# Where a small load is issued: x and the gate's weights in one load ahead of the context's end, or in two behind it

## The chip, the cores and the metric

The kernel runs on one core of a Trainium2 chip. Its time is the device time of one execution in microseconds; three runs of the kernel before gave a median of 773.87 us (773.8 to 774.09). The profile is of one execution, and its span goes from the first to the last recorded instruction.

## What is computed

Two rows x (B = 2, one token each, D = 1024) go through two branches, and a gate mixes them:

```
g   = sigmoid((x * gate_w).sum(-1))
a   = attention(x @ wq, k_cache, v_cache) @ wo     # 32 query heads, 4 kv heads, 32768 keys, head size 128
b   = x + gelu(layernorm(x) @ w3) @ w4              # what is left of the mixer with one token
out = g * a + (1 - g) * b
```

With a single token the shifted mixing of the reference is a sum over zeros, so w1 and w2 are not read. All data are float32. The caches are by far the most of it: 2 x 4 pairs of batch row and kv head, each with 16 MB of keys and 16 MB of values.

## The kernel before

Everything large passes through two buffers of 128 partitions x 64 KB, `ring` (also `flat`, the same memory with flat rows). SP issues every large load, in one written order: wq in two halves, w3 in two halves, then for each of eight pairs two halves of keys and two of values (w4 in two halves ahead of the fifth pair), last wo in four pieces and the `tail` in four. `load` (L212) puts a wait in front of the issue where the buffer must first come free: w3's halves wait for the marks `q0` and `q1` (L249, L250), which PE sets when it has multiplied with the halves of wq.

The only other input is `xg`, 128 partitions x 24 floats: on each partition 8 values of each of the two rows of x and 8 of gate_w. It goes to `xg_sb`. ACT issues its load (L245) inside a critical block (L242 to L245), in which SP also issues the two halves of wq. `tc.close()` and `tc.compile()` (L246, L247) end the tile context; all engines meet there, and the rest of the program is written engine by engine with semaphores set by hand.

What x sets going, in order:

- DVE waits for `got_x` at 16 (L307), forms x * gate_w and the sums over k (L308 to L310).
- PE waits for it too (L338), permutes x (L340) and sums over partitions with a matrix of ones (L344); DVE writes `x_run` and `x_pad` (L315, L319), the mean and the squares (L321 to L325); PE sums again (L346).
- ACT loads the table of its square root ahead of that (L329), then computes the root and the gate's sigmoid (L329, L330); DVE writes `xn_pad` and `xr_pad` for layernorm and the residual.
- PE then runs `project(x_pad, ...)` (L383, matmuls in `columns`, L355): for each half of wq it waits until that half has landed (L361), does 32 matmuls of 512 columns (64 instructions in the profile, each a pair), and marks the end, `q0` and `q1`.

So x stands ahead of PE's use of wq's first half, that use ahead of the mark `q0`, and that mark ahead of SP's issue of w3's first half (L249).

A DMA raises its semaphore by 16 when it has landed. `got_x` is used a second time at the end: the first two pieces of `tail` raise three of these semaphores again, and `came` (L210) holds the values that PE waits for there, 32 for `got_x`.

Of the kernel before, what the change touches and what calls it, by code (L numbers as in the profile page):

```python
# [14 lines left out]
P = 128  # L15
B, D, HQ, HKV, SK, DH, F = 2, 1024, 32, 4, 32768, 128, 3584
REP = HQ // HKV
PAIRS = B * HKV
# [53 lines left out]
def kernel(  # L72
# [52 lines left out]
    nc = tc.nc  # L125
    scale = DH ** -0.5

    def new(name, *shape, parts=P):
        return nc.alloc_sbuf_tensor(name, [parts, *shape], F32).ap()
# [6 lines left out]
    xg_sb = new("xg_sb", KD, 3)  # L136
# [55 lines left out]
    def sem(name):  # L192
        cleared.append(nc.alloc_semaphore(name))
        return cleared[-1]

    stored = nc.alloc_semaphore("stored")
    pe, dve, act, pool = (Line(e, sem(n)) for e, n in (
        (nc.tensor, "pe"), (nc.vector, "dve"), (nc.scalar, "act"), (nc.gpsimd, "pool")))
# [4 lines left out]
    got_x = sem("got_x")  # L203
# [3 lines left out]
    step, own_step, to_pe, pt_in, b_in, e_in, x_in, k1_free = (  # L207
        sem(n) for n in ("step", "own_step", "to_pe", "pt_in", "b_in", "e_in", "x_in", "k1_free"))

    came = ((got_x, 32), (b_in, 16), (pt_in, 16), (k1_free, PAIRS + 16))  # L210

    def load(dst, src, sem, *marks):  # L212
        sp.after(*marks)
        nc.sync.dma_start(dst, src).then_inc(sem, 16)  # L214

    def run(src, j):
        return src[PART * j:PART * (j + 1)].rearrange("i (q w) c -> (i q) (w c)", w=PART)
# [24 lines left out]
    with tc.tile_critical(sync_engine=mybir.EngineType.SP):  # L242
        for j in range(2):
            load(flat[j], run(wq, j), landed[j])
        nc.scalar.dma_start(xg_sb, xg).then_inc(got_x, 16)  # L245
    tc.close()  # L246
    tc.compile()  # L247

# [26 lines left out]
        load(tail[:, 3 * D + i * D // 2:3 * D + (i + 1) * D // 2], run(wo, 1)[:, lo:lo + D // 2], came[2 + i][0])  # L275


    pool.mark(nc.gpsimd.memset(wide, 0.0))
    pool.after((pool.sem, pool.n))
    made = pool.mark(nc.gpsimd.affine_select(  # L280
# [11 lines left out]
    def then(inst):  # L292

        mark = dve.mark(inst)
        dve.after(mark)
        return mark
# [5 lines left out]
    d_perm = dve.mark(last)  # L302
# [1 line left out]
    def over_k(t):  # L304
        return t.rearrange("p (o b) -> p o b", o=1).to_broadcast([P, KD, B])

    dve.after((got_x, 16))  # L307
    then(nc.vector.tensor_mul(xw, xs, xg_sb[:, :, B:B + 1].to_broadcast([P, KD, B])))  # L308
    nc.vector.tensor_reduce(part[:, 0:B], xw.rearrange("p k b -> p b k"), axis=AX.X, op=ALU.add)
    d_part = dve.mark(nc.vector.tensor_reduce(  # L310
# [24 lines left out]
    then(nc.vector.tensor_scalar(rest, gate, -1.0, 1.0, op0=ALU.mult, op1=ALU.add))  # L335
    d_norm = dve.mark(nc.vector.tensor_mul(xr_pad[:, :, ::C // B], xs, over_k(rest)))

    pe.after(d_perm, (got_x, 16))  # L338
    for w in range(PART):
        last = nc.tensor.matmul(tr[1][:, w * KD * B:(w + 1) * KD * B], perm[:, w].rearrange("p i q -> p (i q)"), xs,  # L340
                                start=True, stop=True)
# [314 lines left out]
```

## Time and profile before

| | |
|---|---|
| time, median of 3 runs | 773.87 us |
| profiled execution, its time | 773.87 us |
| its span | 772.3 us |
| PE busy | 431.1 us (56%) |
| DVE busy | 94.6 us (12%) |
| ACT busy | 60.8 us (8%) |
| read from HBM | 331.36 MB, 429 GB/s over the span |

The page gives busy time by engine, 40 slices of the span with the share in tenths, the DMA queues, the chain of work that ended last, and the costliest groups of instructions. In the DMA view a queue's row has its packets, MB and the time that they took as a share of 16 engines over the window asked for; it can be over 100% in a short window, since a packet counts where it starts. In the timeline a row has its start, its length, engine, line, operation, tiles and count, and in brackets the idle time before it and what ended that. "SPq" and "ACTq" are the issues of DMAs, not their transfers.

### The profile page before, as it was taken

The page shows a single profiled execution, that of the slowest core. Times are in us where ns is not written, and L with a number is a line of the kernel's source. Part 1 is how long each engine was busy: PE and PEld are TensorE (multiplying, and loading weights), DVE is VectorE, ACT ScalarE, POOL GpSimd, SP SyncE. Part 2 cuts the span into 40 slices and gives each one's busy share as a digit, 9 for nine tenths or more (in the row PEclk, how much of TensorE's full clock was granted, in tenths as well). Part 3 has the DMA queues.
Part 4 walks back from the last instruction along what each step waited for, and adds up shares of the span by engine and source line. Part 5 has one row for each costly group of instructions (what it writes and reads, how often), then busy time and mean ns, then how long its engine had stood idle before and what let it go on. Part 6 is the DMA issues. An engine that isn't in the chain of part 4 may idle for free. (4 is left out here: it accounts for less than half of the span.)

```text
span 772.3 us, 7548 instructions
## 1 busy us (share of the span) xinstructions
PE 431.1 (56%) x3380; PEld 198.3 (26%) x3380; DVE 94.6 (12%) x267; ACT 60.8 (8%) x145; POOL 3.6 (0%) x12
## 2 busy tenths in 40 slices
PE   1465746454745474656475347454656464547476
PEld 0131413222322232323232113122323131213234
DVE  2010102100210021002100002100210021002110
ACT  1000002000200021002000002000200020002000
POOL 1000000000000000000000000000000000000000
PEclk9976677877687668667867777776776787777779
DMA  9999999999999999999999999999999999999997
GB/s 381 435 435 435 435 435 435 435 429 431 431 435 431 435 435 435 435 435 435 430 428 443 429 435 435 435 435 435 435 435 435 435 435 435 435 435 435 418 426 325
DMA packets 6805, 331.51 MB, mean 429 GB/s; under 512 B 900, under 2 KB 908, under 8 KB 1292
## 3 DMA queue, kind: packets, MB, share of 16 engines
q1 hardware_dynamic: 6634, 331.36, 99.3%
q8 instruction: 8, 0.13, 0.1%
q10 hardware_dynamic: 162, 0.02, 0.0%
q14 instruction: 1, 0.01, 0.0%
HBM read 331.36 MB, written 0.01 MB: 429 GB/s over the span
## 5 line engine op out<-in xcount | busy, mean ns | idle before, releaser
L471 PE MATMUL sc<-load,q_cur 128*32 128x512 f32 x1024 | 146.9, 734 | 133.0 <-PEq L51 133.0
L497 PE MATMUL pv<-load,pt 128*32 128x512 f32 x1024 | 130.9, 669 | 90.3 <-PEq L51 90.3
L471 PEld LDWEIGHTS sc<-load,q_cur 128*32 128x32 f32 x1024 | 52.7, 132 | 221.1 <-issue 219.3
L497 PEld LDWEIGHTS pv<-load,pt 128*32 128x32 f32 x1024 | 39.1, 122 | 172.1 <-issue 172.1
L488 PE MATMUL sc<-wide,p 128*128 128x128 f32 x256 | 44.3, 346 | 22.8 <-PEq L51 22.8
L554 DVE TENSOR_REDUCE mx<-sc 128x1 f32<-128x512 f32 x32 | 21.4, 689 | 287.0 <-PE sc L471 287.0
L538 ACT ACT_TABLE_LOAD x8 | 10.3, 1283 | 488.7 <-ACTq L51 488.7
L488 PEld LDWEIGHTS sc<-wide,p 128*128 128x128 f32 x256 | 39.9, 183 | 30.0 <-issue 30.0
L369 PE MATMUL acc<-load,w_pad 128*32 128x256 f32 x448 | 29.9, 428 | 19.6 <-PEq L51 19.6
L571 DVE COPY pt<-sc 64x256 f32<-64x256 f32 x64 | 25.9, 414 | 75.5 <-PE sc L488 75.0
L544 ACT COPY pt<-sc 64x256 f32<-64x256 f32 x64 | 23.5, 367 | 79.4 <-PE sc L488 77.1
L576 DVE COPY pv_sb<-pv 128x512 f32<-128x512 f32 x16 | 10.3, 686 | 149.6 <-PE tr L503 149.6
L355 PE MATMUL sc<-load,x_pad 128*32 128x512 f32 x128 | 17.9, 722 | 16.3 <-PEq L51 16.3
L369 PEld LDWEIGHTS acc<-load,w_pad 128*32 128x32 f32 x448 | 17.0, 123 | 31.7 <-issue 25.7
L507 PE MATMUL tr<-sel,pv_sb 128*128 128x8 f32 x128 | 18.6, 282 | 11.8 <-PEq L51 11.8
L355 PE MATMUL sc<-load,xn_pad 128*32 128x384 f32 (+1 forms) x128 | 17.4, 711 | 9.3 <-PEq L51 9.3
L538 ACT ACTIVATE p<-sc,bias 128x512 f32<-128x512 f32 x32 | 21.5, 685 | 0.1
L507 PEld LDWEIGHTS tr<-sel,pv_sb 128*128 128x128 f32 x128 | 18.1, 226 | 12.3 <-issue 12.3
L567 DVE COPY p<-p 128x256 f32<-128x256 f32 x32 | 9.4, 294 | 26.7 <-ACT p L538 26.7
L355 PEld LDWEIGHTS sc<-load,x_pad 128*32 128x32 f32 x128 | 5.0, 130 | 28.4 <-issue 28.4
L355 PEld LDWEIGHTS sc<-load,xn_pad 128*32 128x32 f32 x128 | 5.3, 139 | 21.5 <-issue 21.5
L340 PE MATMUL tr<-xg_sb,perm 128*128 128x16 f32 x4 | 1.0, 372 | 13.4 <-DMA xg_sb<-xg 13.4
(86 smaller groups left out, 92.4 us busy)
## 6 DMA issues: line engine op xcount, KB each, us to landing
load<-w SPq DMA_DIRECT2D x4, 7168.0 KB, 27.2
load<-wo SPq DMA_DIRECT2D x1, 7168.0 KB, 29.0
load<-wo SPq DMA_DIRECT2D x1, 4096.0 KB, 17.6
load<-wo SPq DMA_DIRECT2D x1, 2048.0 KB, 22.1
load<-wo SPq DMA_DIRECT2D x1, 1024.0 KB, 24.1
tail<-wo SPq DMA_DIRECT2D x1, 1024.0 KB, 26.1
tail<-wo SPq DMA_DIRECT2D x1, 512.0 KB, 26.9
tail<-wo SPq DMA_DIRECT2D x2, 256.0 KB, 27.1
```

The lines of the kernel that those rows point to most:

```text
L355: last = nc.tensor.matmul(b[C * g:C * g + C, :hi - lo], pad[:, k], t[:, o + lo:o + hi], start=(k == 0), stop=(k == KD - 1))
L369: inst = nc.tensor.matmul(acc[C * g:C * g + C], lhsT, rows[:, g * (D // G):(g + 1) * (D // G)], start=False, stop=last, skip_group_check=True)
L471: last = nc.tensor.matmul(sc[i][C * g:C * g + C], q_cur[:, w, s], ring[j][:, w, o:o + 512], start=(s == 0 and w == 0), stop=(s == 1 and w ...
L488: last = nc.tensor.transpose(sc[k][:, t * P:(t + 1) * P], pair.rearrange("p w q -> p (w q)"), ident)
L497: last = nc.tensor.matmul(pv[C * g:C * g + C], pt[j][w][:, lo:lo + C], ring[j][:, w, o:o + G * DH], start=(j == 0 and w == 0 and t == 0), ...
L507: last = nc.tensor.matmul(tr[1][:, w * REP:(w + 1) * REP], pv_sb[:, s, w].rearrange("p i q -> p (i q)"), sel[:, s], start=(s == 0), stop=( ...
L538: nc.scalar.activation(p[:, i, :, :PART], sc[i].rearrange("p (t q w) -> p t w q", t=NT, w=PART), AF.Exp, bias=bias, scale=scale, accum_out ...
L544: nc.scalar.copy(*halves(1, j, c)).then_inc(pt_in, 1)
L554: last = [nc.vector.reduce_max(out=mx[:, k:k + 1], in_=sc[k], axis=AX.X) for k in ((1, 2) if i == 2 else (i,))][-1]
L567: nc.vector.tensor_copy(p[:, i, :, PART], p[:, i, :, 0]).then_inc(to_pe, 1)
L571: nc.vector.tensor_copy(*halves(0, j, c)).then_inc(pt_in, 1)
L576: last = nc.vector.tensor_copy(pv_sb[:, :, :, i], pv.rearrange("p (s q w) -> p s w q", q=HALF, w=PART))
```

## The change

The load of `xg` leaves the critical block. Behind the end of the context, and behind the written list of SP's loads, ACT issues it as two loads, of partitions 0 to 119 and of 120 to 127, both on `got_x`. The waits for x go from 16 to 32, and the wait at the end on the same semaphore from 32 to 48. SP's list, the order of its loads and all instructions of PE, DVE and POOL are as before. On ACT the two issues now stand behind the context's end and ahead of the first table load.

```diff
-    came = ((got_x, 32), (b_in, 16), (pt_in, 16), (k1_free, PAIRS + 16))
+    came = ((got_x, 48), (b_in, 16), (pt_in, 16), (k1_free, PAIRS + 16))
...
     with tc.tile_critical(sync_engine=mybir.EngineType.SP):
         for j in range(2):
             load(flat[j], run(wq, j), landed[j])
-        nc.scalar.dma_start(xg_sb, xg).then_inc(got_x, 16)
     tc.close()
     tc.compile()
...
+    for rows in (slice(0, 120), slice(120, P)):
+        nc.scalar.dma_start(xg_sb[rows], xg[rows]).then_inc(got_x, 16)
...
-    dve.after((got_x, 16))
+    dve.after((got_x, 32))
...
-    pe.after(d_perm, (got_x, 16))
+    pe.after(d_perm, (got_x, 32))
```

## The prediction

> **What bounds the kernel now.** I read the page's totals and slices first, then the chain that ended last, then the first 51 us of the timeline, and last the DMA view in short windows, because the change touches only the start.
>
> ```profile
> span 772.3 us, 7548 instructions
> DMA  9999999999999999999999999999999999999997
> GB/s 381 435 435 435 435 435 435 435 429 431 431 435 431 435 435 435 435 435 435 430 428 443 429 435 435 435 435 435 435 435 435 435 435 435 435 435 435 418 426 325
> q1 hardware_dynamic: 6634, 331.36, 99.3%
> DMA tail<-wo 4%; PE pv L497 1%; SPq L214 0%; PE sc L378 0%; ACT out L619 0%
> ```
>
> The sixteen DMA engines are full from the first slice to the last: SP's queue q1 alone takes 99.3% of them. The chain ends in the last of its loads. So the time is the length of q1's stream, and an edit matters only if it makes that stream start at another time, run dry, or carry more. The first slice has 381 GB/s where the next ones have 435: 12% of 19.3 us, some 2.4 us at the start in which nothing moves yet.
>
> The x load is small and early. These rows of the timeline carry its way to the stream:
>
> ```profile
> 0.92 0.41 ACTq L245 DMA_DIRECT2D xg_sb<-xg  x1
> 0.96 0.88 SPq L214 DMA_DIRECT2D load<-wq  x2
> 2.91 1.28 ACT L329 ACT_TABLE_LOAD   x1 [2.91 <-PEq L247]
> 13.26 0.17 DVE L308 TENSOR_TENSOR xw<-xg_sb 128x16 f32<-128x16 f32 x1 [6.57 <-DMA xg_sb<-xg]
> 15.94 0.59 PE L346 MATMUL tr<-part,ones 128*128 128x2 f32 x2 [1.16 <-DVE part L325]
> 23.00 9.53 PE L355 MATMUL sc<-load,x_pad 128*32 128x512 f32 x64 [6.48 <-PEq L51]
> 32.59 18.55 SPq L214 DMA_DIRECT2D load<-w  x2
> 42.37 8.39 PE L355 MATMUL sc<-load,x_pad 128*32 128x512 f32 x64 [9.83 <-PEq L51]
> ```
>
> x can be used at 13.26. From there to the end of L346 it takes 15.94 + 0.59 - 13.26 = 3.27 us; PE then idles 6.48 us until wq's first half is there at 23.00. It multiplies for 9.53 us, and its end (32.53) lets SP issue w3's first half at 32.59 into the buffer that came free.
>
> Now the DMA view in windows: what starts in 1.9:3.05, in 5.0:5.7 (the queues' rows of 7.4:8.1 and 9.8:10.5 have the same packets), in 12.3:12.9, in 21.9:22.6, in 41.2:41.9 and in 0:42. Each row of digits cuts its window into 40 slices, so a digit that isn't 0 says when packets start: in the second, slices 4 to 35 of 0.0175 us, 5.07 to 5.62. q10 is ACT's queue, and up to 42 us it carries nothing but x.
>
> ```profile
> q1 hardware_dynamic: 16, 1.05, 254.3%
> q10 hardware_dynamic: 80, 0.01, 10.9%
> ...
> DMA  0000900090000009099090909900990000090000
> ...
> q1 hardware_dynamic: 16, 1.05, 345.4%
> q10 hardware_dynamic: 16, 0.00, 1.7%
> ...
> DMA  0009000900000000990909090099009090000090
> ...
> q10 hardware_dynamic: 16, 0.00, 1.5%
> ...
> q1 hardware_dynamic: 32, 1.05, 346.7%
> ...
> DMA  0000000900009000009909099909900990000090
> ...
> q10 hardware_dynamic: 144, 0.01, 0.4%
> ```
>
> x is 144 packets: 128 rows and 16 completions, so 8 + 1 on each of 16 engines. 80 of them, five per engine, go beside the first 16 packets of wq; then comes one per engine each time that an engine ends a packet of wq: at 5.07 to 5.62, in 7.4:8.1, in 9.8:10.5, and its completions at 12.34 to 12.88 (slices 3 to 38 of 0.015 us). A packet of wq takes 3.454 x 16 x 0.7 / 16 = 2.418 us. So **a small packet that shares the engines with the stream waits 2.42 us for each turn**, and x was early only because five of its nine turns were over before the stream began, thanks to an issue 0.04 us ahead of SP's. In 21.9:22.6 q1 has 32 packets, 16 of data and the 16 completions of wq's first half. The last row of digits is the same for wq's second half: it ends between 41.32 and 41.88 (slices 7 to 38), and w3 must be there by then or the engines stand still.
>
> **The change, part by part.** *Removed:* one DMA issue (0.41 us) on ACT at 0.92. SP's two issues at 0.96 are in the same place and wait for nothing of ACT's. The 144 packets cost the engines 0.4% of 42 us = 0.17 us each, spent now or later. The first wq packets took 2.543 x 1.15 = 2.92 us in the mean against 2.418; if x's neighbourhood causes that, up to 0.5 us comes back, or nothing. I take 0.
>
> *Moved:* the load goes behind the context's end. There ACT's first instruction starts at 2.91 (the table load, L329). Both x issues stand ahead of that load now; it moves back by two issues, and its user waited long for it:
>
> ```profile
> 16.76 0.20 ACT L329 ACTIVATE rstd<-rstd 128x2 f32<-128x2 f32 x1 [12.57 <-DVE rstd L327]
> 770.50 1.11 ACTq L620 DMA_DIRECT2D out<-out  x1
> ```
>
> An issue on ACT costs 0.41 (x) to 1.11 us (the result's), so the two end at 3.7 to 5.1 and the table at 6.4 at the latest: hidden under 12.57 us of waiting, and uncovered only if the table took longer than x. DVE and PE have the same instructions, with a 32 for a 16 in two waits, and the tail's first wait (48 for 32) counts the same events: nothing.
>
> *What the move costs x.* Issue to first packet was about 1.05 us (0.92 to some 1.97; the window 1.9:2.0 holds 16 packets of x and none of wq):
>
> ```profile
> q10 hardware_dynamic: 16, 0.00, 9.7%
> ```
>
> So x's first packet can go at 2.91 + 1.05 = 3.96 or later, inside the first wq packet, which ends at 5.1 to 5.6. The head start is gone and every turn costs 2.42 us.
>
> How many turns? 120 rows on 16 engines put 8 rows on some (120/16 = 7.5), plus a completion: 9 turns. The 8-row load shares engines with them (9 + 1 + 1 = 11) unless it goes whole to an engine that the first one leaves free (again 9). x was spread as thinly as its rows allow, so I take 11; the other end is 9, that is 4.84 us less. The Trainium skill ("DMA: Bandwidth & Descriptors", section "Why a DMA increments its semaphore by 16 and not by 1") says that a copy runs on the largest number of engines up to 16 that divides its rows: by that, an estimate, 15 engines with 8 rows and 8 engines with one, which gives 11 as well.
>
> At which packet end does the first turn come? If an engine picks its next packet only as it ends one, at the first (5.1 to 5.6); if it has picked wq's second packet by 3.96 to 4.9, at the second. The stream runs without gaps although a first packet costs 0.5 us more, so picking is at least 0.5 us ahead; x comes 0.7 to 1.1 us ahead. The slowest of eight engines decides. I take the second end; the first and the third are the bounds. One turn is saved where q1's own completion comes between two wq packets (21.9:22.6), so eleven turns from the second end finish at the 2 + 9 = 11th: 5.6 + 10 x 2.42 = 29.8. With 13.26 - 12.88 = 0.38 us to DVE, x is usable at **30.2, 16.9 us later**.
>
> *What covers that.* First PE's idle time: 23.00 - 16.53 = 6.47 us. Then the lead of w3's issue: at 32.59, where the stream needs it by 41.32 - 1.05 = 40.27: 7.68 us. Together 14.15, that is, x usable by 27.4 costs nothing. So 16.9 - 14.15 = **2.8 us in which the engines stand dry**, and nothing gives that back, since the stream has no other hole. Two corrections bound it. After a dry spell the first packets may cost 0.5 us more again (up to 3.3). And PE's 9.53 us holds a slow beginning, as these two rows of its lines in 22.9:27 and 29:32 show:
>
> ```profile
> L355 PE MATMUL sc<-load,x_pad 128*32 128x512 f32 x20 | 4.5, 1059 | 6.5 <-PEq L51 6.5
> ...
> L355 PE MATMUL sc<-load,x_pad 128*32 128x512 f32 x36 | 4.0, 592 | 0.0
> ```
>
> After an idle spell a matmul takes 1059 ns, later 592. With the chain L340 to L346 right ahead of it PE may be quick sooner, as in the second half's 8.39: 1.1 us less (down to 1.7). Later work has room: wq's second half is multiplied at 43 instead of 42.37, and what follows waits for w3, which is later by the same 2.8.
>
> *Sum.* The profiled execution took 773.87 us (span 772.3), which is also the median of the three runs: 773.87 + 2.8 = **776.7 us**, with 775.5 to 777.3 for this case.
>
> **Rivals.**
>
> 1. *x's turns start one packet earlier* (first end, last turn 27.4, usable at 27.8): 0.4 us over the cover, minus up to 1.1, plus up to 0.5: 773.9 to 774.8. This is the case that is not slower, together with nine turns; it decides from x usable at 27.4, and the forecast lies 2.8 us on the wrong side of it. For it: an engine that picks late. Against: the stream's lack of gaps. 0.20, and 0.02 for nine turns.
>
> 2. *Several small packets go in one turn.* Five went together at the start. If that is no head start but a habit of the engines (five in a first turn, or in each), eleven packets take three to seven turns, the last at 5.6 + 7 x 2.42 = 22.6 at the latest, x is usable by 23.0, inside the cover, and the time stays: 773.5 to 774.0. Against: rounds two to four had one each, though the rest of x was surely queued. 0.13. The Trainium skill ("DMA: Bandwidth & Descriptors", section "Queues, rings and completion order") speaks for more of this: an engine drains a whole packet of typically 9 to 17 descriptors from one ring before it switches; by that x would be in within one turn. The trace does not agree: 16 packets of q10 per 16 packets of q1.
>
> 3. *Later still.* If the engines have picked two to four packets of wq ahead, the turns begin at the third to fifth end: 2.4 us more each, 779.1 to 784 (where rival 4 begins). Against: 256 KB picked ahead by each engine is much. 0.14, most of it at the third end.
>
> 4. *x stands behind wq's second half altogether*, if the packets of both queues reach the engines in the order of issue. x then comes when the stream runs dry, at 41.9, is usable at 42.3, and w3 is issued at 42.3 + 3.27 + 9.53 = 55.1: 42.3 - 27.4 = 14.9 us over, 784 to 789. No case can be worse, since a dry stream lets x through. Against: SP issues loads close behind each other without a stall; nothing shows ACT's beside them. 0.06.
>
> ```profile
> 741.09 1.85 SPq L214 DMA_DIRECT2D tail<-wo  x4
> ```
>
> 5. *The stream starts better without x.* Up to 0.5 us from the first packets, 1 us if all sixteen began together, and up to the half of SP's 0.88 us if two issues run quicker without ACT's beside them: 772.3 to 773.6, with x in time as in rivals 1 and 2. Against: ACT's issue is over at 1.33 and SP's takes 0.44 us each wherever it stands. 0.05, counted as faster.
>
> That the change doesn't do what it says is rival 2 or 1: a later issue that nothing waits for.
>
> **How the numbers follow.** Forecast 0.40, rival 1 with nine turns 0.22, rival 2 0.13, rival 3 0.14, rival 4 0.06, rival 5 0.05. A measurement of this kernel can tell about 0.2%, 1.55 us, from no change. Slower: 0.40 + 0.14 + 0.06 = 0.60. Same: 0.22 + 0.13 = 0.35. Faster: 0.05. The range reaches from rival 2's 773.5 to 780.0, over the third end of rival 3; it leaves out rival 4, rival 5 and the deeper half of rival 3, 0.18. The likeliest case alone has 775.5 to 777.3.
>
> **What would show it.** In the profile after: ACT's two issues at 2.9; 16 or 15 packets of q10 in each window of 2.42 us, from 7.5 on, eleven rounds, the last to 29.8; DVE L308 (L310 by the new numbering) at 30.2; PE's first L355 group at 33.5 and not 23.0; SP's w3 issue at 43; a hole of 2 to 3 us in q1 between 41.9 and 45; every later load late by as much, the span 775.1. DVE at 27.8 or before and no hole is rival 1 or 2; a first turn after 10 us is rival 3; no q10 packet ahead of 22 is rival 4. The forecast is wrong if w3's issue still comes before 40.3.

## The result, and the profile after

The changed kernel takes 776.62 us (median of six runs, 776.07 to 777.61) against 773.98 us for the kernel before: a ratio of 1.0037, 95% interval 1.0027 to 1.0047. That is 2.64 us more; 776.7 was forecast. The profiled execution took 776.80 us (span 775.2), 2.93 us more than the one of before.

The page after: span, DMA slices, the large queue, the chain.

```profile
span 775.2 us, 7546 instructions
DMA  9999999999999999999999999999999999999997
GB/s 379 433 383 430 433 434 433 434 434 433 433 433 433 436 436 436 436 436 440 433 432 435 430 436 433 433 436 433 433 433 433 433 433 433 433 433 433 419 432 314
q1 hardware_dynamic: 6634, 331.36, 99.1%
DMA tail<-wo 4%; PE pv L499 1%; SPq L214 0%; PE sc L380 0%; ACT out L621 0%
```

The stream still bounds the kernel, with the same packets and bytes, and the chain still ends in its last load. One slice stands out: the third, 38.8 to 58.1 us, has 383 GB/s where it had 435. That is (435 - 383) / 435 of 19.4 us, 2.3 us of transfer that did not take place. The first slice has 379 instead of 381, so the start gained nothing. The window 1.9:3.05 has the first wq packets, now without x beside them:

```profile
q1 hardware_dynamic: 16, 1.05, 279.2%
```

They take 2.792 x 1.15 = 3.21 us in the mean, where they took 2.92 beside x. So x was not what made them slow, and they end no earlier than before (at 5.0 to 5.6, before at 5.1 to 5.6).

The timeline after, the rows that answer to those of before:

```profile
0.95 0.86 SPq L214 DMA_DIRECT2D load<-wq  x2
2.83 0.98 ACTq L278 DMA_DIRECT2D xg_sb<-xg  x2
3.84 1.28 ACT L331 ACT_TABLE_LOAD   x1 [3.84 <-issue]
30.09 0.18 DVE L310 TENSOR_TENSOR xw<-xg_sb 128x16 f32<-128x16 f32 x1 [23.50 <-DMA xg_sb<-xg]
32.78 0.59 PE L348 MATMUL tr<-part,ones 128*128 128x2 f32 x2 [1.16 <-DVE part L327]
33.30 16.20 PE L357 MATMUL sc<-load,x_pad 128*32 128x512 f32 x128
42.36 7.51 SPq L214 DMA_DIRECT2D load<-w  x2
```

x is usable at 30.09 instead of 13.26. PE no longer idles ahead of wq's first half; it starts at 33.30 instead of 23.00 and goes through both halves in one piece, and SP issues w3 at 42.36 instead of 32.59.

In the DMA view, these are the rows of q10 in the windows 7.3:8.1, 21.9:22.6, 24.3:25.1, 29.1:29.9 and 0:42:

```profile
q10 hardware_dynamic: 15, 0.00, 1.4%
...
q10 hardware_dynamic: 30, 0.00, 3.2%
...
q10 hardware_dynamic: 15, 0.00, 1.1%
...
q10 hardware_dynamic: 8, 0.00, 0.6%
...
q10 hardware_dynamic: 151, 0.01, 0.3%
```

151 packets are 120 + 15 and 8 + 8: the first load runs on 15 engines with 8 rows each, the second on 8 with one row. The first turn comes in 7.3:8.1, the end of wq's second packet. In 21.9:22.6, where the completions of wq's first half stand between two wq packets, x has two turns in one: that is the turn which the prediction counted as saved. The first load's completions come in 24.3:25.1, the second's in 29.1:29.9.

And the hole. The first block has the packet count of the window 41.2:42.0, then the digits and q1's row of 43.0:45.5, all of the kernel after; the second has q1's row in 43.4:44.1 of the kernel before:

```profile
DMA packets 16, 0.00 MB, mean 0 GB/s; under 512 B 16, under 2 KB 16, under 8 KB 16
...
DMA  0000099999090090090000000000000000000900
...
q1 hardware_dynamic: 16, 0.92, 112.7%
```

```profile
q1 hardware_dynamic: 16, 0.92, 302.3%
```

In 41.2:42.0 only the completions of wq are left, 16 packets with no data. The first packets of w3 start from 43.3 on (slice 5 of 0.0625 us), the last of them at 45.3, on an engine that ran a packet of another queue (q8, instructions) ahead of it. By the packets' own records wq's last ones end at 41.64 in the mean of the 16 engines and w3's first ones start at 43.59, so 1.95 us lie between in the mean. And they begin slowly: the first 16 packets of w3 take 1.127 x 2.5 = 2.82 us in the mean; the second 16 of the kernel before, in the running stream, took 3.023 x 0.7 = 2.12. That is 0.70 us more in the mean, and 1.95 + 0.70 = 2.65 us together.

### The profile page after: what moved, and what is told of

It is laid out like the page before. It is cut to its first block, busy times and chain, and to the rows that moved or that the text cites. A ratio compares the mean times of both kernels' runs of the same rounds, so it can differ in the third digit from the quotient of the medians.

```text
span 775.2 us, 7546 instructions
## 1 busy us (share of the span) xinstructions
PE 433.1 (56%) x3380; PEld 198.3 (26%) x3380; DVE 94.6 (12%) x267; ACT 60.8 (8%) x145; POOL 3.6 (0%) x12
## 5 line engine op out<-in xcount | busy, mean ns | idle before, releaser
L473 PE MATMUL sc<-load,q_cur 128*32 128x512 f32 x1024 | 148.5, 741 | 128.9 <-PEq L51 128.9
L490 PEld LDWEIGHTS sc<-wide,p 128*128 128x128 f32 x256 | 39.6, 182 | 30.0 <-issue 29.9
L371 PE MATMUL acc<-load,w_pad 128*32 128x256 f32 x448 | 32.6, 457 | 18.6 <-PEq L51 18.6
L342 PE MATMUL tr<-xg_sb,perm 128*128 128x16 f32 x4 | 1.0, 372 | 30.2 <-DMA xg_sb<-xg 30.2
L357 PE MATMUL sc<-load,x_pad 128*32 128x512 f32 x128 | 16.1, 660 | 0.1
L342 PEld LDWEIGHTS tr<-xg_sb,perm 128*128 128x128 f32 x4 | 0.9, 322 | 30.2 <-issue 30.2
## 6 DMA issues: line engine op xcount, KB each, us to landing
load<-wo SPq DMA_DIRECT2D x1, 1024.0 KB, 24.3
tail<-wo SPq DMA_DIRECT2D x2, 256.0 KB, 27.4
```

The source lines that it names most:

```text
L357: last = nc.tensor.matmul(b[C * g:C * g + C, :hi - lo], pad[:, k], t[:, o + lo:o + hi], start=(k == 0), stop=(k == KD - 1))
L371: inst = nc.tensor.matmul(acc[C * g:C * g + C], lhsT, rows[:, g * (D // G):(g + 1) * (D // G)], start=False, stop=last, skip_group_check=True)
L473: last = nc.tensor.matmul(sc[i][C * g:C * g + C], q_cur[:, w, s], ring[j][:, w, o:o + 512], start=(s == 0 and w == 0), stop=(s == 1 and w ...
L490: last = nc.tensor.transpose(sc[k][:, t * P:(t + 1) * P], pair.rearrange("p w q -> p (w q)"), ident)
```

## The experiments

Theory: each small packet of a queue waits for the end of one 2.42 us packet of the stream (a turn; "first end" and "second end" are the ends of wq's first and second packet on an engine). The number of turns, and the end at which they start, set when x is usable; past 27.4, with PE at 9.53 us for wq's first half, the stream runs dry and the time grows. Rivals: the place behind the context's end costs by itself, or the split does, or the loss isn't in the hole.

**One load at the new place.**

```diff
-    for rows in (slice(0, 120), slice(120, P)):
-        nc.scalar.dma_start(xg_sb[rows], xg[rows]).then_inc(got_x, 16)
+    nc.scalar.dma_start(xg_sb, xg).then_inc(got_x, 16)
```

> One load of 128 rows at the new place: the split alone is undone. Turns (the theory of the prediction: one small packet per engine at each end of a 2.42 us packet of wq, from the second end on): 9 turns instead of 11, so the completions come at 24.3 to 25.0, two turns earlier than 29.2 to 29.7, and x is usable at 25.3, inside the cover that ends at 27.4. No hole, 773.9 (773.6 to 774.3). Rival (the place costs, not the number of turns: a load behind the context's end makes the stream run dry by itself): 776 to 777, as with two loads.

Measured: 773.96 us, ratio 1.0000 (0.9991 to 1.0010). Its timeline:

```profile
25.37 0.18 DVE L309 TENSOR_TENSOR xw<-xg_sb 128x16 f32<-128x16 f32 x1 [18.77 <-DMA xg_sb<-xg]
...
38.09 14.07 SPq L214 DMA_DIRECT2D load<-w  x2
```

x is usable 12.1 us later than before, and that costs nothing: w3 is issued 2.2 us ahead of the cover's end at 40.27. With one load the place costs x 12.1 us and the kernel nothing; the two turns that the split adds are what goes over.

**Two loads of 120 and 8 at the old place**, in two runs. The edit is shown against the kernel before; the waits for x are those of the change.

```diff
-        nc.scalar.dma_start(xg_sb, xg).then_inc(got_x, 16)
+        for rows in (slice(0, 120), slice(120, P)):
+            nc.scalar.dma_start(xg_sb[rows], xg[rows]).then_inc(got_x, 16)
```

> The two loads of 120 and 8 rows at the old place, inside the critical block: the move alone is undone. Turns: the first load keeps its head start of five turns, the second comes behind it in the same queue, so six turns of 2.42 us from the first end: completions of the second load at about 17.2 to 17.8, x usable near 18.1, under PE's idle time until 23.0. 773.9 (773.6 to 774.3). Rival (two loads on fewer engines cost by themselves): 775 or more.

Measured: 775.42 us, ratio 1.0021 (1.0011 to 1.0031), two of ten at 774.1, the others from 775.08 to 776.79. The expectation missed: there was no head start. Timeline, and q10 in the windows 5.0:5.8 (in 1.9:5.0 it has no packet at all):

```profile
0.92 1.02 ACTq L246 DMA_DIRECT2D xg_sb<-xg  x2
...
27.57 0.18 DVE L310 TENSOR_TENSOR xw<-xg_sb 128x16 f32<-128x16 f32 x1 [20.79 <-DMA xg_sb<-xg]
30.77 8.76 PE L357 MATMUL sc<-load,x_pad 128*32 128x512 f32 x64
39.60 10.38 SPq L214 DMA_DIRECT2D load<-w  x2
```

```profile
q10 hardware_dynamic: 15, 0.00, 1.4%
```

Though issued at 0.92 as before, x has its first turn only at the first packet end and goes through all eleven turns from there: usable at 27.57, 0.2 us past the cover, and one turn ahead of the change, whose turns start at the second end. The profiled execution (774.09) has no hole, since PE needed only 8.76 us for wq's first half. The same kernel again:

> The two loads of 120 and 8 at the old place once more, since its times spread from 774.06 to 776.79 while its profile (774.09) has no hole. x was usable at 27.57 there, 0.2 us past the cover's end, with w3 issued at 39.60 because PE ran the first half of wq in 8.8 us and not 9.5. If the time is set by that edge: a profile with 775 or more has w3's issue after 40.3 and a hole behind wq, either because PE took 9.5 us or because x came one turn (2.42 us) later. If the loss is elsewhere, the hole is missing in a run of 775 as well.

Measured: 773.98 us in one run, with x at 27.65, PE 8.73 us, w3 issued at 39.65 and no hole. So both profiles are of executions of 774 us and show why those lose nothing; an execution of 775 or more of this kernel was not profiled. Inconclusive here; the next kernels supply it.

**Two loads of 64**, at the old place and at the new one.

```diff
-            for rows in (slice(0, 120), slice(120, P)):
+            for rows in (slice(0, 64), slice(64, P)):
```

> Two loads at the old place, of 64 and 64 rows, each over all 16 engines, instead of 120 and 8. With 120 and 8 x had lost its head start of five turns (first packet at 5.04 instead of 1.97). If a load on fewer than 16 engines comes to the engines later, this one has the head start: the first load's five packets per engine at 2 to 3, the rest in up to five turns, x usable at 13 to 16. If any split loses it: ten turns from the first end, x usable near 25. Either lies under the cover: 773.9.

Measured: 775.71 us in one run. No head start either: x came in ten turns from the second end, usable at 27.86. PE took 9.69 us and w3 was issued at 40.83, past the cover. The expected 773.9 was wrong with it.

> Two loads of 64 rows at the new place: 10 turns from the second end, x usable at 27.8, as in the two of 64 at the old place (27.86, 775.71), which had ten turns from the second end as well. If only the turn count and the end from which it starts matter, and not the place: 774.5 to 776.0, with w3's issue at 40 to 41, depending on PE's pace in wq's first half (8.7 to 9.7 us in the runs so far), and first packets of w3 0.4 to 0.7 us longer than the rest. If the place costs by itself: as with 120 and 8, 776.6.

Measured: 775.12 us, ratio 1.0015 (1.0005 to 1.0025), two of ten at 773.7 to 773.8, the others from 774.86 to 776.80. The profiled execution took 775.59:

```profile
27.73 0.17 DVE L311 TENSOR_TENSOR xw<-xg_sb 128x16 f32<-128x16 f32 x1 [22.06 <-DMA xg_sb<-xg]
...
30.93 9.78 PE L358 MATMUL sc<-load,x_pad 128*32 128x512 f32 x64
40.78 9.02 SPq L214 DMA_DIRECT2D load<-w  x2
```

Same turns, same x, same issue of w3 as at the old place: for two loads of 64 the place doesn't matter. (For 120 and 8 it does: the turns start one end later at the new place, 776.62 against 775.42 us.) And x within 0.3 us of the split's 27.57, with PE a whole us slower, lands at 775.6: at the edge, PE's pace decides between no loss and 1.7 us. That is the likely reason for the spread of the loads of 120 and 8 at the old place; it is argued from these two kernels.

**More turns: four loads, eight loads** (the waits for x count all of them; the second kernel has 8 for 4).

```diff
+    for i in range(4):
+        rows = slice(i * P // 4, (i + 1) * P // 4)
+        nc.scalar.dma_start(xg_sb[rows], xg[rows]).then_inc(got_x, 16)
```

> Four loads of 32 rows at the new place: 2 rows and a completion on each engine four times, 12 turns, one more than with 120 and 8. Turns: last completions 2.42 us later, x usable at 32.5, the hole 2.4 us longer: 779.0 (778.3 to 779.7). Rival (place or split cost, turns don't matter): 776 to 777, or less since every load is spread over all engines.

Measured: 779.50 us, ratio 1.0072 (1.0055 to 1.0089), x usable at 32.52, w3 issued at 44.95.

> Eight loads of 16 rows at the new place: 1 row and a completion on each engine eight times, 16 turns. The 16th turn is at the end of wq itself, 41.3 to 41.9, if no load is issued too late for its turn (an issue takes about 0.46 us, a turn 2.42). x usable at 42.3, w3 issued at about 55, 785 to 789. This is also the ceiling: with wq over, nothing holds x back any more. Rival: loads spread over all engines are served quicker, under 780.

Measured: 789.39 us in one run, just above what was expected. Its timeline:

```profile
42.42 0.18 DVE L311 TENSOR_TENSOR xw<-xg_sb 128x16 f32<-128x16 f32 x1 [35.83 <-DMA xg_sb<-xg]
...
45.63 16.56 PE L358 MATMUL sc<-load,x_pad 128*32 128x512 f32 x128
55.40 7.19 SPq L214 DMA_DIRECT2D load<-w  x2
```

One turn more made x 2.43 us later (32.52 - 30.09), and the 16th fell on the end of wq, the ceiling. Seven profiled executions together, each with its own time. "Worked out" is 773.87 plus what w3's issue is past 40.27 plus, where it is past, 0.7 us for the slow first packets (measured in the changed kernel alone, as above):

| kernel | turns | x usable | w3 issued | worked out | time |
|---|---|---|---|---|---|
| one load, new place | 9 | 25.37 | 38.09 | 773.9 | 773.98 |
| 120 and 8, old place | 11 | 27.57 | 39.60 | 773.9 | 774.09 |
| two of 64, new place | 10 | 27.73 | 40.78 | 775.1 | 775.59 |
| two of 64, old place | 10 | 27.86 | 40.83 | 775.1 | 775.71 |
| 120 and 8, new place (the change) | 11 | 30.09 | 42.36 | 776.7 | 776.80 |
| four of 32, new place | 12 | 32.52 | 44.95 | 779.3 | 779.16 |
| eight of 16, new place | 16 | 42.42 | 55.40 | 789.7 | 789.39 |

One number, the issue of w3, gives the time of all seven within 0.6 us.

**Two queues.** The 8 rows go to POOL's queue with a semaphore of their own, for which DVE and PE wait too; the 120 stay with ACT.

```diff
+    nc.scalar.dma_start(xg_sb[:120], xg[:120]).then_inc(got_x, 16)
...
+    nc.gpsimd.dma_start(xg_sb[120:], xg[120:]).then_inc(got_rest, 16)
```

> The changed kernel with the 8 rows issued by POOL, behind its memsets, instead of by ACT. Turns, counted per queue: the 120 rows need 9 turns of ACT's queue from the second packet end, completions 24.3 to 25.0; the 8 rows take two turns of a queue of their own, done by 16. x usable at 25.3, inside the cover: no hole, 773.9 (773.6 to 774.3). Rival (all small packets of an engine share one turn between two packets of wq, whatever their queue): 11 turns, 30.1, 776.6.

Measured: 773.87 us, ratio 1.0001 (0.9991 to 1.0010). Timeline, and the queues in 12:15.3:

```profile
25.30 0.18 DVE L311 TENSOR_TENSOR xw<-xg_sb 128x16 f32<-128x16 f32 x1 [19.61 <-DMA xg_sb<-xg]
...
37.83 14.09 SPq L215 DMA_DIRECT2D load<-w  x2
```

```profile
q1 hardware_dynamic: 32, 2.10, 146.5%
q10 hardware_dynamic: 30, 0.00, 0.7%
q0 software_dynamic: 32, 0.00, 0.6%
```

Within two ends of wq packets (32 of q1), ACT's queue had its two turns on 15 engines and POOL's queue all 32 of its packets: a turn belongs to a queue. Here the split stands at the new place and nothing is lost: neither costs by itself.

**Is the hole the whole loss?** First, a useful transfer is put there: the tail's first 1 MB, whose buffer is free from the start, on a semaphore of its own.

```diff
+    load(tail[:, :2 * D], run(wo, 0)[:, PART * KF // 4 * D:], early)
     load(flat[0][:, :PART * 2 * F], run(w3, 0), landed[0], at("q0"))
...
-    load(tail[:, :2 * D], run(wo, 0)[:, half * D:], came[0][0])
```

> The changed kernel, with the first 1 MB of the tail issued right behind wq instead of at the end (the buffer is free from the start). x is as late as before it, but the stream has 2.41 us more to carry until w3 must be there. If the hole is the whole cost, it shrinks from 2.7 to 0.3 us, at most 0.7 more for a restart: 774.0 to 775.0; the end may lose up to 1 us since 1 MB less lies behind wo's last piece there. If something else makes the kernel slower (more packets, another start of the stream), it stays at 776.6.

Measured: 775.75 us, ratio 1.0023 (1.0013 to 1.0034), 0.9 us less than the change and more than expected. The chain of this kernel ends differently:

```profile
768.95 1.10 PE acc L372 x16
...
770.08 0.43 DVE so_far L604
...
770.56 2.24 PE sc L381 x104
...
772.82 0.44 ACT out L622 x2
```

PE's work behind wo's last piece is now the end, no longer covered by the transfers that were moved. The same move in the kernel before shows its price:

> The control of the run with the tail's first 1 MB moved: the same move in the kernel before, where there is no hole to fill. x usable at 13.3, no hole. If that move costs at the end (there PE became the end of the chain and the last store came 1.6 us behind the last load), 774.5 to 775.5 here, and what the changed kernel still loses at the start in that run is the difference, under 1 us. If the move costs nothing at the end, 773.9, and the hole was not filled in that run.

Measured: 775.25 us, ratio 1.0017 (1.0008 to 1.0027), and its chain ends in the same work of PE: 1.35 us from the end alone. So the start of the other kernel still loses 775.75 - 775.25 = 0.5 us in the median, instead of 2.64. No single run of it lies there, though: four of the eight took 775.13 to 775.26, as long as the control, so they lost nothing at the start, and four took 776.24 to 776.72, some 1.3 us more. The profiled one (776.72) is of the second kind; its w3 was issued at 42.67, at the very edge, since the extra 2.41 us move the cover's end to 42.68. The kernels with 120 and 8 at the old place and with two of 64 at the new one leave the same gap between a few runs without loss and the others.

Then 1 MB is loaded there in addition, and again at the end as before:

```diff
+    load(tail[:, :2 * D], run(wo, 0)[:, PART * KF // 4 * D:], early)
...
-    load(tail[:, :2 * D], run(wo, 0)[:, half * D:], came[0][0])
+    load(tail[:, :2 * D], run(wo, 0)[:, half * D:], came[0][0], (early, 16))
```

> The changed kernel with 1 MB more to load: the tail's first piece is loaded right behind wq and, as before, once more at the end. The end is untouched. The extra transfer takes 2.41 us of the stream. If the engines stand dry for 2 to 3 us behind wq, it fits in there and costs nothing: 776.6 (776.0 to 777.3). If the stream has no hole and the loss lies elsewhere, 1 MB more is 2.41 us more: 779.0.

Measured: 777.74 us, ratio 1.0047 (1.0030 to 1.0064), between the two and above the expected 776.0 to 777.3. Of the 2.41 us of transfer 1.3 are hidden and 1.1 are not. Its timeline:

```profile
33.20 16.74 PE L359 MATMUL sc<-load,x_pad 128*32 128x512 f32 x128
43.15 7.19 SPq L215 DMA_DIRECT2D load<-w  x2
```

w3 was issued at 43.15, not 42.36: PE took some 9.9 us for wq's first half instead of 9.0. With the cover's end at 40.27 + 2.41 = 42.68, that leaves 0.5 us of hole and the 0.7 of slow first packets: 773.87 + 2.41 + 1.2 = 777.5, where the profiled execution took 777.83. So idle time can be filled; the slow restart stays as soon as w3 is late at all. The expectation had left that and PE's pace out.

**A single load a little later at the old place**, by eight empty instructions ahead of the issue.

> The kernel before, with eight empty instructions ahead of ACT's issue, so that it comes some tenths of a us behind SP's first and not 0.04 us ahead of it. If the five early turns are a head start (the prediction's reading): none of them is left, nine turns from the first or second end, x usable at 22.9 or 25.3, and the time stays 773.9 under the cover. If five in the first turn are a habit of the engines (rival 2 of the prediction): five per engine together at the first turn, x usable by 15.5.

Measured: 773.73 us, but the issue was at 0.92 as before and x usable at 13.14 with its five early turns. The edit did not move what it was to move; the run tells nothing on the question.

## Why the prediction was right

- *What bounds the kernel*: the stream, unbroken but for one hole. The third slice shows it alone.
- *Eleven turns*: right, by the packet counts (15 and 8 engines, and two turns in one at the end of wq's first half) and by the seven kernels of the table. With nine turns at the same place the loss is gone.
- *From the second end*: right, by the first q10 window. It was a choice between neighbours that the trace of before didn't settle; with it x was worked out at 30.2 and came at 30.09. The reason given, how far ahead an engine picks its packets, is not shown: the two loads of 64, issued at 0.92 and so two us earlier, began at the second end as well. That the choice hit is in part luck.
- *The cover*: right. For the issue of w3 it ends at 40.27: 39.65 cost nothing and 40.78 did. The 27.4 for x holds for PE at 9.53 us only; with 8.76, x at 27.57 cost nothing.
- *The 2.8 us dry*: the sum held, its parts did not. The engines were idle for 1.95 us in the mean, because PE took 9.0 us and not 9.53 (the correction that was named as a bound), so that w3 was issued at 42.36 and not at 43. The first packets took 0.70 us longer (taken at 0, bounded at 0.5, which was too low). The two errors cancel; that the time came within 0.1 us of the forecast is luck.
- *The start gains nothing without x*: right; the first slice has 379 for 381, and the first wq packets took 3.21 us without x beside them.
- *The rivals*: the first turn was not at the first end here (it was with 120 and 8 at the old place, and x came 2.5 us earlier). Several packets in one turn: no, 15 per round for the first load and 8 for the second, but for the 30 at the end of wq's first half. Later ends: no. Behind wq altogether: no, but the kernel with eight loads, whose x came with wq's end, shows its price: 789.39, where 784 to 789 was worked out.
- *Five early turns as a head start of 0.04 us*: half right. It is lost at the new place, as said. But two loads at the old place, issued at the same 0.92, lost it too, so the start of the issue is not all of it.

## What to carry to other kernels

Beside the stream of these runs, which fills the engines with packets of 2.42 us, a small load cost one packet time of the stream for each of its rows per engine and one for each completion. So count rows per engine plus loads in one queue: splitting within a queue made x later, and the same split over two queues did not. (A row was 96 bytes in every run; what a larger one costs was not tried.) Follow such a load to the issue that it holds up in the end, and work out the slack up to that issue: 12 us of delay were free here, 17 were not. At the edge, expect scatter, and count the slow restart of the stream on top of the hole.

## What the hardware showed that was not expected

- After 1.95 us without work the first packets of w3 took 2.82 us in the mean instead of 2.12. In the other kernels with a late w3 they took 2.54 to 2.76, whatever the length of the hole (14.9 us with eight loads), so this belongs to the price; and wq's first packets took 2.91 to 3.21 instead of 2.42 at the start of every execution.
- ACT's issue of x took 0.40 to 0.41 us for 128 rows, 0.66 to 0.70 for 120 rows, 0.29 for 8, and 0.58 to 0.61 for each of two loads of 64. The loads with 0.41 at 0.92 had five turns ahead of wq (three kernels), those with a longer first issue had none (two kernels). It fits that an issue which ends behind SP's first loses the race, but no run separates the two, and why the loads of 64 started one end later than the 120 stays open.
- PE took 8.6 to 9.9 us for the same 64 matmul instructions of wq's first half, from one kernel to another. The granted clock was 1.00 there in all of them, so it doesn't explain this. The difference lies in how long the slow beginning lasts: the first 4 us hold 28 or 29 matmuls in the four executions with 8.6 to 8.8 us and 24 or 25 in the others. What sets that was not tried; it is enough to decide at the edge between 774 and 775.6 us.
